# A fused attention and FFN kernel: the value products of a unit placed behind the first-layer products of their step, one half of P at a time

## The chip, the cores and the metric

The kernel runs on one core of one Trainium2 chip. The metric is device time in microseconds for one execution of the whole program.

## The reference

An attention whose mask comes from a hash, and a feed-forward network on its output, all in 32-bit floats. There are 4 batches of 8 heads, 768 positions, 64 features per head; the FFN goes from 512 to 2048 and back.

```python
q_bits = (einsum('bhsd,dk->bhsk', q, proj) > 0)      # 6 bits; k_bits likewise
mask = q_bucket[:, :, :, None] == k_bucket[:, :, None, :]
scores = where(mask, q @ k^T / 8, -1e9)
scores = scores - max(scores)
attn = exp(scores); attn = attn / (sum(attn) + 1e-09)
x = (attn @ v)  ->  [3072 tokens, 512]
h = x @ w_in
g = h * clip(h + 3, 0, 6) / 6
out = g @ w_out
```

## The kernel before, in words

**Precision.** TensorE multiplies a reduced 32-bit format, so operands are kept as a high part (rounded, written by ScalarE) and a low part (the rest, written by VectorE or POOL), and a product is made of two or three partial products that are summed in PSUM.

**Attention.** A score tile g holds 128 queries against the 768 keys of a head; there are 192 of them, six to a head. TensorE makes it with four products (L387, L389) into the PSUM tile s. VectorE copies it out and finds the row's extreme (`lowest`, L396), ScalarE takes the exponential (`exponential`, L408); the result is the tile p, the P of the title. The value products need P with the keys on the partitions. For tiles below GT = 102 TensorE transposes p (L418). From tile 102 on VectorE transposes blocks in place (`flip`, L429), SyncE's queue writes the tile to DRAM (fd) and reads it back in the other order into one of two buffers, spare and px (`move`).

**Halves.** `split_p` makes the high part ph on ScalarE (L475) and the low part pl. The 768 keys are cut in two halves of three key blocks: c = 0, whose low part VectorE makes (L479), and c = 1, whose low part POOL makes (L477; POOL's half). The halves of one unit are tiles of their own; there are two buffers for ph and two for pl, so a half of the next unit takes the buffer of the same half of this one.

**Units.** Two score tiles, 2u and 2u + 1, are a unit u: 256 queries. Its value products multiply the split v of the head (stationary) with ph and pl (moving): 2 halves x 3 key blocks x 2 parts = 12 products of 128x256, all summed into one PSUM tile, acc. `values_whole` (L505, its products at L513) issues all twelve; `values` (L500) issues half a unit at a time in the earlier part of the program. ScalarE copies acc out (`output`, L547), from where it goes to DRAM (xs) by SyncE's and POOL's queues.

**The FFN** works on chunks of 256 tokens, with 16 steps fc of 128 hidden features each. A step has 12 first-layer products of 128x256 (`gemm1`, L661) into the PSUM tile h; ScalarE's ReLU (L683) and VectorE's multiplication (L684), both from h; the split of the result into gb, high on ScalarE (L689) and low on VectorE (L690); and 6 second-layer products of 128x512 (`gemm2`, L699, L700, L704) into po, where L699 and L700 need the high part and L704 the low one. gb of a step is made at the start of the next step, and used in it.

**The order.** On TensorE, VectorE, ScalarE and POOL the order in which the code is written is the order of execution; the order on SyncE's queue is made by a scheduler. The part that the change concerns is `beside_ffn(k)`, called for k = 101 to 194: one step of attention and one step of the FFN side by side. `fill` is a coroutine over the FFN; `go("A")` to `go("D")` let it run when it has come to that stage: A splits gb, B issues the first-layer products, C the second-layer products of the step before and the gate, D side work. In a step from k = 102 on, TensorE's queue held before the change: in odd steps the 12 value products of unit (k - 3) / 2; the first-layer products; in one odd step of each head six hash products (L334 to L336); the second-layer products; the score products of tile k + 3; in some steps two transposes for the normalisation of a chunk (L587). Even steps have no value products. In step k the halves of tile k - 1 are split: POOL's half right after the exponential, the other half behind the ReLU.

**PSUM.** acc, h, the hash tile z and the normalisation tile rt come from `bank()`, which deals four banks out in turn. A tile waits for whoever still reads the bank that it is given.

Of the kernel before, what the change touches and what calls it, by code (L numbers as in the profile page):

```python
# [43 lines left out]
def lsh_attention_moe(  # L44
# [11 lines left out]
    B, H, D, S = qkT.shape  # L56
# [4 lines left out]
    QT = HW // P  # L61
# [31 lines left out]
    def bank(shape, name: str, tag: str | None = None):  # L93

        nonlocal turn
        if tag is None:
            tag = ("pt", "pu")[turn % 2]
            turn += 1
        return ps.tile(shape, F32, name=name, tag=tag, bufs=2)
# [132 lines left out]
    GT = GF + FT  # L232
# [179 lines left out]
    pts, parts = {}, {}  # L412
# [92 lines left out]
    def values_whole(u: int):  # L505
        vv = vvs[2 * u // KT]
        acc = accs[u] = bank([P, 2 * P], f"acc{u}")
        both = [parts.pop((u, c)) for c in range(2)]
        first, end = (0, 1, 0), (1, 0, QT - 1)
        for part in range(2):  # L510
            for c in (1, 0):
                for x in range(QT):
                    nc.tensor.matmul(  # L513
                        acc[:], lhsT=vv[:, c * QT + x], rhs=both[c][part][:, x],
                        start=(part, c, x) == first, stop=(part, c, x) == end,
                    )

    adds, fresh = [], []

# [552 lines left out]
    vnext = 0  # L1072

    def value_whole():
        nonlocal vnext
        values_whole(vnext // 2)
        vnext += 2

    def value_half():
        nonlocal vnext  # L1080
        u, c = divmod(vnext, 2)
        vnext += 1
        values(u, c)
        return c == 1
# [14 lines left out]
    with tc.manual_schedule(engines={ET.PE, ET.DVE, ET.Activation, ET.Pool}):  # L1099
        split_qk(0, None)  # L1100
        hash_qk(0)
        bits(0)
        scale_q(1)
        split_v(0)
        for x in range(3):
            ahead(0, x)
        for _ in range(2):
            cv(0)
        def go(part: str):
            if stage == part:  # L1110
                next(fill, None)

        through = []

        def beside_ffn(k: int):

            nonlocal paced, stage, held
            held = False  # L1120
            if k < GT:
                for c in range(2):
                    transp(k, c)
                exponential(k + 1)
            for _ in range(2):
                u = vnext // 2
                if u < NS // 2 and (2 * u < GT or k % 2 and k >= 2 * u + 3):
                    if vnext % 2 == 0 and k >= GT:
                        value_whole()
                        through.append(u)  # L1130
                        break
                    if value_half():
                        through.append(vnext // 2 - 1)
                if k < GT:
                    break
            behind = (k - 1 + LA) % KT == 4
            if GT <= k < NS - 2 and not behind:
                lowest(k + 2)
            go("A")
            if GT <= k < NS - 2 and behind:  # L1140
                lowest(k + 2)
            if k < GT:
                for c in range(2):
                    split_p(k, c, False)
                split_lows()
                while through:
                    output(through.pop(0))
                flip(k + 1)
            if k + 2 < NS:
                if k < GT:  # L1150
                    lowest(k + 2)
                    assert len(side) <= 2
                    opening.pop()()
                if k == GT:
                    go("B")
                    go("C")
                exponential(k + 2)
            paced = True
            multiply()
            if k + 2 < NS:  # L1160
                flip(k + 2)
            split = GT <= k - LT < NS
            if split:
                split_p(k - LT, 1, False)
            go("B")
            if k == NS + LT:
                homes.clear()
            while through and (through[0] < vnext // 2 - 1 or k % 2 == 0 or k < GT):
                output(through.pop(0))
            hashed = k + LA < NS and (k + LA) % KT == 4 and (k + LA) // KT + 1 < NJ  # L1170
            if hashed:
                hash_qk((k + LA) // KT + 1)
            if split:
                amid.append(lambda: (split_p(k - LT, 0, False), split_lows()))
            go("C")
            while amid:
                amid.pop()()
            split_lows()
            if hashed:
                bits((k + LA) // KT + 1)  # L1180
            if k + LA < NS:
                lead(k + LA)
            if moves:
                moves.pop(0)()
            if GT <= k + 1 < NS:
                move(k + 1)

            place_in_chunk = (k - GT) % NFC
            if subs and (k % 2 and (k < GT or place_in_chunk != NFC - 1) or k > GT and place_in_chunk == 0):
                subs.pop(0)()  # L1190
            go("D")
            if k % KT in (1, 3):
                add()

        for k in range(NS + LT + 2):
            if k >= GT - 1:
                beside_ffn(k)
                continue
            end = GB if k < GB else NS
            i, t = divmod(k, KT)  # L1200
            if k == HK - XE:
                lent += lents[cc3:]
            if k == GB:
                lent.clear()
            if k == GF - 6:
                load_first_x()
            if k == HK:
                late["x"] = sp.tile([P, S], F32, name="late", tag="raw", bufs=1)
            for c in range(2):
                transp(k, c)  # L1210
            if k + 1 < end:
                exponential(k + 1)
            if k + 2 < end:
                lowest(k + 2)
            if k == GB:
                next(first)
                pair_turn = 0

            third = True
            whole = False  # L1220
            for _ in range(1 if k != HK else 2):
                if vnext < k - k % 2:
                    whole = value_half()
            held = k >= GF - 2
            if held:
                next(fill, None)
            if whole and k >= GF:
                output(vnext // 2 - 1)
                whole = False

            hashed = k >= GF and (k + LA) % KT == 2
            after = hashed or k >= GF and (k + LA) % KT == 3
            if k >= GF and k + LA < end and not after:
                lead(k + LA)
            for c in range(2):
                split_p(k, c, third)
            split_lows()
            multiply()
            held = False
            if (k < GF or after) and k + LA < end:  # L1240
                if hashed:
                    if (k + LA) // KT + 1 < NJ:
                        hash_qk((k + LA) // KT + 1)
                        bits((k + LA) // KT + 1)
                    next(fill, None)
                lead(k + LA)
            if k == GB - 2:
                hash_qk((GB - 1) // KT + 1)
                bits((GB - 1) // KT + 1)
            if whole:  # L1250
                output(vnext // 2 - 1)
            if k >= GF - 2 and not hashed:
                next(fill, None)
            if k < GB:
                for f in early_steps[k]:
                    f()

            if k < HK and t == 1 and i:
                with tc.issue_after(last.ins):
                    load_w(i)  # L1260
            if k == HK:
                add()
                late_x()
                with tc.issue_after(last.ins):
                    get_qk(H + 2)
                    for n in range(WE, WL):
                        load_w(n)
            if k + 1 == GB:
                first = first_ffn(lambda part: ahead(GB, part))
                next(first)  # L1270
                for _ in range(2):
                    whole = value_half()
                output(vnext // 2 - 1)
                next(first)
        paced = False
        assert vnext == NS and not through
        add()
        add()
        for _ in fill:
            pass  # L1280
# [47 lines left out]
```

## Time and profile before

| | |
|---|---|
| median of 3 runs | 975.36 us (973.79 to 977.28) |
| the profiled execution's own time | 973.11 us |
| its span, first to last instruction | 971.3 us |
| instructions | 19460 |
| granted TensorE clock, mean | 0.998 |
| value products at L513 | 276 on ph and 276 on pl, from 396.2 to 812.4 us |
| bytes moved by DMA | 152.06 MB |

The rows in the prediction are of one profiled execution. A row of the timeline has the start in microseconds from the span's start, the duration, the engine, the line of the program, the operation, output and inputs, the shape, the type and how many instructions were merged into the row; in square brackets stands the idle time of that engine just before, and what ended it. PE is TensorE's matmul, PEld its weight load, DVE is VectorE, ACT ScalarE, POOL GpSimd, SP SyncE. Matmuls are pipelined: each starts before the one ahead of it has ended, and a matmul's end is modelled. A row of the waits has the waiting engine, its line, what it waited for, and then the total, the number of times and the longest wait.

### The profile page before, as it was taken

How to read it: one execution, taken by the hardware profiler on the slowest of the kernel's cores; microseconds unless marked ns; L12 is line 12 of the kernel's file. 1: busy time of each engine (PE TensorE's matmuls, PEld its weight loads, DVE VectorE, ACT ScalarE, POOL GpSimd, SP SyncE). 2: the span in 40 equal slices, each digit the busy share in tenths (PEclk: the TensorE clock that was granted, in tenths of full speed). 3: DMA queues.
4: the chain of work that ended last, by engine and by line, in shares of the span. 5: the costliest groups of instructions: out<-in, count | busy, mean ns of one | idle time of the engine just before them, and what ended most of it. 6: DMA issues, size and time to landing. Idle time of an engine off the chain costs nothing.

```text
span 971.3 us, 19460 instructions
## 1 busy us (share of the span) xinstructions
PE 948.0 (98%) x6306; PEld 873.6 (90%) x6306; DVE 723.5 (74%) x1470; ACT 625.0 (64%) x1421; POOL 473.6 (49%) x582
## 2 busy tenths in 40 slices
PE   8999999999999999899999999999999999999997
PEld 7999888999989999799899899989899899889896
DVE  7999988888569999877878878878777874342422
ACT  6898875655478988667766666666666664333332
POOL 6777744665537776455555545555545432000000
PEclk9999999999999999999999999999999999999999
DMA  3567579100035554787898788788887772101000
GB/s 117 140 156 188 131 224 377 58 1 1 6 119 119 115 142 112 192 252 233 238 267 234 231 256 241 230 267 236 243 258 233 211 227 71 44 1 44 1 22 22
DMA packets 113613, 152.06 MB, mean 157 GB/s; under 512 B 13876, under 2 KB 82612, under 8 KB 113512
## 3 DMA queue, kind: packets, MB, share of 16 engines
q1 hardware_dynamic: 108472, 144.79, 48.8%
q0 software_dynamic: 5040, 6.03, 5.3%
q8 instruction: 50, 0.82, 0.4%
q14 instruction: 51, 0.42, 0.2%
HBM read 77.34 MB, written 54.00 MB: 135 GB/s over the span
## 4 chain that ended last, share of the span: by engine, by line
PE 79%; DVE 8%; DMA 4%; ACT 4%; issue 3%; POOL 1%; SPq 1%; ACTq 0%; DVEq 0%; POOLq 0%
PE h L661 25%; PE acc L500 6%; PE po L704 6%; PE po L699 6%; PE po L700 6%; PE acc L513 6%; PE pt L418 5%; PE s L389 5%; PE s L387 5%; DMA spare<-fd 2%; DVE p L396 2%; DVE pl L479 2%; ACT ph L475 1%; SPq L78 1%; DVE qq L352 1%
## 5 line engine op out<-in xcount | busy, mean ns | idle before, releaser
L408 ACT ACTIVATE p<-p,m 128x768 f32<-128x768 f32 x192 | 180.2, 939 | 113.4 <-DVE p L396 105.2
L396 DVE TENSOR_SCALAR_CACHE_REDUCE p<-s 128x768 f32<-128x768 f32 x192 | 182.7, 952 | 24.9 <-PE pt L418 12.4
L684 DVE SCALAR_TENSOR_TENSOR h<-g,h 128x256 f32<-128x256 f32 x192 | 81.1, 423 | 102.0 <-ACT g L683 99.0
L683 ACT ACTIVATE g<-h,three 128x256 f32<-128x256 f32 x192 | 91.2, 475 | 94.9 <-PE h L661 94.0
L661 PE MATMUL h<-xh,w 128*128 128x256 f32 x1024 | 146.8, 282 | 0.0
L661 PEld LDWEIGHTS h<-xh,w 128*128 128x128 f32 x1024 | 134.9, 188 | 4.2 <-ACT xh L650 0.6
L429 DVE STREAM_TRANSPOSE p<-p 128x768 f32<-128x768 f32 x90 | 88.1, 979 | 65.2 <-ACT p L408 65.1
L477 POOL TENSOR_TENSOR pl<-spare,ph 128x384 fp32r<-128x384 f32 x45 | 45.8, 1018 | 127.3 <-ACT ph L475 71.4
L479 DVE TENSOR_TENSOR pl<-pt,ph 128x384 fp32r<-128x384 f32 x196 | 100.0, 550 | 4.0 <-ACT ph L475 3.5
L387 PE MATMUL s<-kk,qq 76*128 76x384 f32 x384 | 100.5, 343 | 2.0 <-ACT kk L357 1.5
L389 PE MATMUL s<-kk,qq 128*128 128x384 f32 x384 | 100.4, 343 | 0.0
L700 PE MATMUL po<-w,gb 128*128 128x512 f32 x250 | 98.4, 393 | 0.0
L699 PE MATMUL po<-w,gb 128*128 128x512 f32 x250 | 98.3, 393 | 0.0
L475 ACT CAST ph<-pt 128x384 fp32r<-128x384 f32 x196 | 86.1, 474 | 14.3 <-PE pt L418 13.0
L216 POOL TENSOR_TENSOR w<-wr,w 128x128 fp32r<-128x128 f32 x128 | 71.9, 593 | 45.2 <-ACT w L210 41.9
L418 PE MATMUL pt<-ident,p 128*128 128x128 f32 x612 | 86.2, 275 | 1.9 <-DVE pl L479 1.1
L689 ACT CAST gb<-h 128x256 fp32r<-128x256 f32 x141 | 52.4, 372 | 54.5 <-DVE h L684 26.8
L661 PE MATMUL h<-xl,w 128*128 128x256 f32 x512 | 81.2, 280 | 0.0
L418 PEld LDWEIGHTS pt<-ident,p 128*128 128x128 f32 x612 | 72.5, 141 | 8.9 <-PE pt L418 1.5
L704 PE MATMUL po<-w,gb 128*128 128x512 f32 x250 | 78.6, 395 | 1.5 <-DVE gb L690 1.5
L318 POOL TENSOR_TENSOR kk<-raw,qq 64x192 fp32r<-64x192 f32 (+1 forms) x73 | 65.4, 920 | 25.1 <-ACT qq L304 21.7
L387 PEld LDWEIGHTS s<-kk,qq 76*128 76x128 f32 x384 | 66.6, 190 | 11.7 <-ACT kk L357 2.0
(153 smaller groups left out, 2150.9 us busy)
## 6 DMA issues: line engine op xcount, KB each, us to landing
fd<-p SPq DMA_DIRECT2D x90, 384.0 KB
spare<-fd SPq DMA_DIRECT2D x180, 96.0 KB
px<-fd SPq DMA_DIRECT2D x180, 96.0 KB
kk<-qq SPq DMA_DIRECT2D x62, 192.0 KB
wr<-in_w_in SPq DMA_DIRECT2D x16, 512.0 KB
wr<-in_w_out SPq DMA_DIRECT2D x16, 512.0 KB
raw<-in_qkT SPq DMA_DIRECT2D x19, 384.0 KB
vr<-in_v SPq DMA_DIRECT2D x32, 192.0 KB
```

What stands on the lines that cost most here:

```text
L387: nc.tensor.matmul(s[:, c, :HW], lhsT=q1[:KM, us], rhs=half(k1[:KM], c), start=True, stop=False)
L389: nc.tensor.matmul(s[:, c, :HW], lhsT=q2[:, us], rhs=half(k2, c), start=False, stop=True)
L396: nc.vector.tensor_scalar(out=pr_[:], in0=s[:, :, :HW], scalar1=CAP, scalar2=None, op0=ALU.min, op1=ALU.min, accum_out=m[:],)
L408: nc.scalar.activation(pr_[:], pr_[:], AF.Exp, bias=m[:], scale=-1.0, accum_out=sms[b][:, t, h : h + 1])
L418: nc.tensor.transpose(pt[:, x], probs[g][0][:, c, x * P : (x + 1) * P], ident[:])
L475: nc.scalar.copy(hi, pt)
L479: lows.append(lambda: engine.tensor_sub(lo, pt, hi.bitcast(F32)))
L661: nc.tensor.matmul(hp, lhsT=wi[:, wp, wc], rhs=x[cc][xp], start=(k == 0 and cc == 0), stop=(k == 2 and cc == NCC - 1),)
L683: nc.scalar.activation(r[:], hp, AF.Relu, bias=three[:], scale=1.0)
L699: nc.tensor.matmul(po[u], lhsT=gh[:, us], rhs=wo[:, 0], start=(fc == 0), stop=False)
L700: nc.tensor.matmul(po[u], lhsT=gh[:, us], rhs=wo[:, 1], start=False, stop=False)
L704: nc.tensor.matmul(po[u], lhsT=gl[:, us], rhs=wo[:, 0], start=False, stop=(fc == NFC - 1))
```

## The change

`values_whole` no longer issues the twelve products itself; it allocates acc and returns a function that issues one half: its three high products, then its three low ones. `value_whole` puts the work on a list, `rest`. For the one unit whose score tiles lie below GT (unit 50) it runs at once, at its old place. For the other 45 units, 51 to 95, it runs behind `go("B")`, so behind the first-layer products of the same step; POOL's half (c = 1) goes first, then the other. The split of POOL's half of the next tile, which was written ahead of `go("B")`, is written behind it, because it reuses the buffers that the moved products read.

```diff
     def values_whole(u: int):
         vv = vvs[2 * u // KT]
         acc = accs[u] = bank([P, 2 * P], f"acc{u}")
-        both = [parts.pop((u, c)) for c in range(2)]
         first, end = (0, 1, 0), (1, 0, QT - 1)
-        for part in range(2):
-            for c in (1, 0):
+
+        def half(c: int):
+            both = parts.pop((u, c))
+            for part in range(2):
                 for x in range(QT):
                     nc.tensor.matmul(
-                        acc[:], lhsT=vv[:, c * QT + x], rhs=both[c][part][:, x],
+                        acc[:], lhsT=vv[:, c * QT + x], rhs=both[part][:, x],
                         start=(part, c, x) == first, stop=(part, c, x) == end,
                     )
+
+        return half
...
     def value_whole():
         nonlocal vnext
-        values_whole(vnext // 2)
+        u = vnext // 2
+
+        def whole():
+            half = values_whole(u)
+            for c in (1, 0):
+                half(c)
+
+        rest.append(whole)
+        if vnext < GT:
+            rest.pop()()
         vnext += 2
+
+    rest = []
...
             split = GT <= k - LT < NS
+            go("B")
+            while rest:
+                rest.pop()()
             if split:
                 split_p(k - LT, 1, False)
-            go("B")
             if k == NS + LT:
                 homes.clear()
```

On TensorE at unit 59 (step k = 121), before the change: s123 is the score tile of the step before, ph59_1 and pl59_1 are POOL's half of the unit, ph59_0 and pl59_0 the other, h1_1_3 is the first layer of the FFN step, z21 the hash of head 21.

```order
L387 MATMUL s123_6721<-kk_20_6143,qq_20_6144 128x384 x2
L389 MATMUL s123_6721<-kk_20_6143,qq_20_6144 128x384 x2
L513 MATMUL acc59_6731<-ph59_1_6637,vv19_6407 128x256 x3
L513 MATMUL acc59_6731<-ph59_0_6663,vv19_6407 128x256 x3
L513 MATMUL acc59_6731<-pl59_1_6638,vv19_6407 128x256 x3
L513 MATMUL acc59_6731<-pl59_0_6664,vv19_6407 128x256 x3
L661 MATMUL h1_1_3_6758<-xh1_1_6546,w6_2339 128x256 x8
L661 MATMUL h1_1_3_6758<-xl1_1_6547,w6_2339 128x256 x4
L334 MATMUL z21_0_6771<-qq_21_6534,pjl_74 108x384
```

And the same place with the change (line numbers behind the diff are higher, so L513 became L514 and L661 became L664):

```order
L387 MATMUL s123_6721<-kk_20_6143,qq_20_6144 128x384 x2
L389 MATMUL s123_6721<-kk_20_6143,qq_20_6144 128x384 x2
L664 MATMUL h1_1_3_6741<-xh1_1_6546,w6_2339 128x256 x8
L664 MATMUL h1_1_3_6741<-xl1_1_6547,w6_2339 128x256 x4
L514 MATMUL acc59_6754<-ph59_1_6650,vv19_6407 128x256 x3
L514 MATMUL acc59_6754<-pl59_1_6651,vv19_6407 128x256 x3
L514 MATMUL acc59_6754<-ph59_0_6663,vv19_6407 128x256 x3
L514 MATMUL acc59_6754<-pl59_0_6664,vv19_6407 128x256 x3
L334 MATMUL z21_0_6771<-qq_21_6534,pjl_74 108x384
```

The twelve value products moved behind the twelve first-layer products, and POOL's low part moved ahead of the other half's high part. The orders on ScalarE, VectorE and POOL are the same as before, instruction by instruction. On SyncE's queue twelve places differ by a transfer or two; this is the difference at step k = 114, where fd116 is the write of a transposed tile, xs2 that of a unit's output y18_0, and spare and px are the buffers that transposed tiles are read into:

```order
 L78 DMA spare_5091<-fd114_6173 32x4x192 x4
 L78 DMA raw21_6326<-in_qkT 64x768 x2
+L78 DMA fd116_6296<-p116_6288 128x768
 L78 DMA xs2_127<-y18_0_6190 64x512
-L78 DMA fd116_6296<-p116_6288 128x768
-L78 DMA px_5555<-fd115_6236 32x4x192 x4
-L78 DMA fd117_6364<-p117_6356 128x768
+L78 DMA px_5555<-fd115_6223 32x4x192 x4
+L78 DMA fd117_6351<-p117_6343 128x768
```

Here the write of the transposed tile went ahead of the write of y; the rows of px and fd117 differ only in the numbers of their buffers.

## The prediction

> **What bounds the kernel now.** I read the page first, then the busy time of the stage that the change touches (microseconds 412 to 814), then that stage's waits, then the timeline around single units. The page's first part:
>
> ```profile
> PE 948.0 (98%) x6306; PEld 873.6 (90%) x6306; DVE 723.5 (74%) x1470; ACT 625.0 (64%) x1421; POOL 473.6 (49%) x582
> ```
>
> TensorE is the bound; no other engine is near. What can be won is only time in which TensorE itself stands. The stage by itself, from the view of busy time by stretch (span, PE, PEld, DVE, ACT, POOL, then granted clock, DMA share, GB/s):
>
> ```profile
> 412.00:814.00 402.00, 397.54 (x2591) 367.90 (x2592) 313.87 (x601) 267.01 (x625) 208.69 (x269) 1.00 0.81 237
> ```
>
> The granted clock is 1.00, so no time hides there. PE shows 4.5 us of idle time, and the waits of this stage (total, times, longest) say where most of it is, and how often VectorE has to wait for TensorE:
>
> ```profile
> DVE p L396 <- PE s L389: 8.2, 21, 0.6
> ...
> PEld acc L513 <- ACT ph L475: 6.0, 12, 1.7
> ...
> PE acc L513 <- ACT ph L475: 4.5, 9, 1.5
> ```
>
> TensorE's idle time lies ahead of the value products (L513), which wait for ScalarE's high part of P. Here is a unit without such a wait (59), and VectorE's wait for a score tile in the even step before it:
>
> ```profile
> 481.12 0.96 DVE L396 TENSOR_SCALAR_CACHE_REDUCE p<-s 128x768 f32<-128x768 f32 x1 [0.42 <-PE s L389]
> ...
> 483.19 0.98 DVE L429 STREAM_TRANSPOSE p<-p 128x768 f32<-128x768 f32 x1 [0.76 <-ACT p L408]
> ...
> 483.46 0.36 ACT L547 COPY y<-acc 128x256 f32<-128x256 f32 x1
> ...
> 484.07 0.52 PE L389 MATMUL s<-kk,qq 128*128 128x384 f32 x2
> ...
> 484.43 0.88 PE L513 MATMUL acc<-ph,vv 128*128 128x256 f32 x6
> ...
> 485.86 1.10 PE L661 MATMUL h<-xh,w 128*128 128x256 f32 x8
> ...
> 487.04 0.50 ACT L475 CAST ph<-spare 128x384 fp32r<-128x384 f32 x1
> ...
> 487.53 0.48 ACT L683 ACTIVATE g<-h,three 128x256 f32<-128x256 f32 x1
> ...
> 488.31 0.40 PE L699 MATMUL po<-w,gb 128*128 128x512 f32 x1
> ```
>
> From first value product to first first-layer product: 485.86 - 484.43 = 1.43 us for twelve products, 0.12 each. Now unit 66, with two rows of the step pair before it:
>
> ```profile
> 541.49 0.63 PE L661 MATMUL h<-xl,w 128*128 128x256 f32 x4
> ...
> 542.22 0.48 ACT L683 ACTIVATE g<-h,three 128x256 f32<-128x256 f32 x1 [0.43 <-PE h L661]
> ...
> 548.55 0.52 PE L389 MATMUL s<-kk,qq 128*128 128x384 f32 x2
> ...
> 549.41 1.00 POOL L477 TENSOR_TENSOR pl<-px,ph 128x384 fp32r<-128x384 f32 x1 [4.00 <-ACT ph L475]
> 549.47 0.59 PE L513 MATMUL acc<-ph,vv 128*128 128x256 f32 x3 [0.39 <-ACT ph L475]
> ...
> 549.86 0.51 ACT L475 CAST ph<-px 128x384 fp32r<-128x384 f32 x1
> ...
> 550.40 0.56 DVE L479 TENSOR_TENSOR pl<-px,ph 128x384 fp32r<-128x384 f32 x1
> 550.42 0.62 PE L513 MATMUL acc<-ph,vv 128*128 128x256 f32 x3 [0.36 <-ACT ph L475]
> ...
> 551.59 1.10 PE L661 MATMUL h<-xh,w 128*128 128x256 f32 x8
> ...
> 551.97 0.36 ACT L689 CAST gb<-h 128x256 fp32r<-128x256 f32 x1
> ...
> 552.99 0.39 PE L699 MATMUL po<-w,gb 128*128 128x512 f32 x1
> ```
>
> In unit 59 the first value product follows 0.36 us after the first of the two score products (484.07), so unit 66 should have begun at 548.91; it began 0.55 us late and then took 551.59 - 549.47 = 2.12 us instead of 1.43: together 1.24 us, where the idle column shows 0.39 + 0.36. I use the distance from start to start, since the next product's start is what the path feels. By the idle column's 4.5 us the gain would be 2 us after what comes back below, and the time 973.
>
> **The change, part by part.** *Waits removed.* The 45 moved units, first and last:
>
> ```profile
> 412.03 1.31 PE L513 MATMUL acc<-ph,vv 128*128 128x256 f32 x6 [0.57 <-ACT ph L475]
> ...
> 413.92 0.28 PE L661 MATMUL h<-xh,w 128*128 128x256 f32 x1
> ...
> 811.09 0.87 PE L513 MATMUL acc<-ph,vv 128*128 128x256 f32 x6
> ...
> 812.51 0.75 PE L661 MATMUL h<-xh,w 128*128 128x256 f32 x5
> ```
>
> Over them, (start of the first first-layer product) - (start of the first value product) - 1.43 sums to 9.7 us. Ten units follow a pair of transposes and need 1.50 without any wait (456.31 to 457.82 below), so 0.7 of it is no wait: 9.0. Ahead of the first product, units 51, 66 and 90 wait 0.73, 0.55 and 0.54: 1.8. Gross: **10.8 us**. Seven units (51, 63, 66, 74, 75, 87, 90) hold 7.4 of it.
>
> Do the waits go? The moved products start 1.43 us later against ScalarE, and are ordered POOL's half high, POOL's half low, other half high, other half low: operands are needed at +1.43, +1.79, +2.14 and +2.50. Take unit 66, its start at 548.91: POOL's low part ends at 550.41 (needed 550.70), ScalarE's other high part at 550.37 (needed 551.05), VectorE's low part at 550.96 (needed 551.41). All in time, in one of the worst three units.
>
> *What is late next.* TensorE now reaches the second-layer products (L699) earlier by what it no longer waits, and their operand gb comes from ScalarE, which is not earlier. In unit 66 gb is there 0.66 us before its use (551.97 + 0.36 against 552.99), and TensorE is 1.24 us ahead, more with what it carries from units 63 and 64: 0.6 to 1.0 comes back. Unit 75:
>
> ```profile
> 632.26 0.51 PE L513 MATMUL acc<-ph,vv 128*128 128x256 f32 x3
> ...
> 633.07 0.37 ACT L547 COPY y<-acc 128x256 f32<-128x256 f32 x1 [1.10 <-DMA xs<-y]
> ...
> 634.25 0.56 DVE L479 TENSOR_TENSOR pl<-px,ph 128x384 fp32r<-128x384 f32 x1
> 634.27 0.63 PE L513 MATMUL acc<-ph,vv 128*128 128x256 f32 x3 [1.50 <-ACT ph L475]
> ...
> 634.85 0.36 ACT L689 CAST gb<-h 128x256 fp32r<-128x256 f32 x1
> 635.45 1.10 PE L661 MATMUL h<-xh,w 128*128 128x256 f32 x8
> ...
> 636.85 0.39 PE L699 MATMUL po<-w,gb 128*128 128x512 f32 x1
> ```
>
> It loses 635.45 - 632.26 - 1.43 = 1.76, because ScalarE waits for a transfer; the margin of gb is 1.64 and the lead would be 1.76 plus 0.6 from unit 74: 0.7 comes back there, and 0.3 in the step after. VectorE regains about 0.4 of lateness per pair of steps (8.2 us over 21 waits), so leads under that die out. For two more units (70, 90) I put 0.4 together. Given back: 0.8 + 1.0 + 0.4 = 2.2, say **2.4**; bounds 0 (all engines follow) and 7.4 (all seven late units only move their wait).
>
> *ScalarE's cast behind the moved products.* The next unit's high part for POOL's half reuses the buffer that the first three moved products read. In unit 59 this cast starts at 487.04, 2.61 after the unit. The products' result: +1.43, three products 0.24 to the third's start, and from a product's start to ScalarE's use 0.38 (the fourth of the products from 541.49 starts at 541.84, L683 at 542.22): +2.05. Covered by 0.56; nothing. Behind that cast stand the ReLU (L683), the other cast and gb, and their readers on VectorE. The ReLU itself starts at +3.10 right behind the cast, so an earlier h brings nothing in such a unit. A rule speaks against this part of the change: the Trainium skill (PSUM — Partial Sum Buffer, section "Engine vs sequencer instructions") states that ScalarE's queue is strict first in, first out and that matmuls complete in program order, so a cast that waits for products moved back by 1.43 us stops all of ScalarE. The trace agrees in unit 75 above, where one late copy (L547) holds what follows; by the rows the cast is not late and the term is 0, and where it were late the second rival gives the time.
>
> *Banks.* In ten units, where transposes take banks too, the first-layer products now wait for the copy of the unit before (L547) out of acc. In unit 56:
>
> ```profile
> 454.99 0.36 ACT L547 COPY y<-acc 128x256 f32<-128x256 f32 x1
> ...
> 456.31 0.96 PE L513 MATMUL acc<-ph,vv 128*128 128x256 f32 x6
> ...
> 457.82 1.10 PE L661 MATMUL h<-xh,w 128*128 128x256 f32 x8
> ```
>
> It ends 0.96 before; these units have little lead (0.3 at most of their own): nothing, 0 to 0.3 each, up to 2 us in all.
>
> *Queues.* The orders of ScalarE, VectorE and POOL stay as they are, POOL's transfers too. On SP some neighbours change place; where the write of a transposed tile (fd) goes ahead of that of y, y waits for the transpose: it ends at 484.17, the copy at 483.82, so 0.35 us. The next copy into a y buffer is a whole pair of steps off: nothing.
>
> *Sum.* 10.8 - 2.4 = 8.4 us. The profiled execution took 973.11 (span 971.3) and would take 964.7; the median of the runs shown is 2.25 above it, so the forecast is 975.36 - 8.4 = **967.0 us**.
>
> **Rivals.** *The wait moves on.* If ScalarE and VectorE, not TensorE's order, set the pace in the late units, the seven give back all: 10.8 - 7.4 = 3.4, so 972.0. For it: the casts in 66 and 75 are late because ScalarE had other work or a transfer to wait for, which stays. Against: only 66 and 75 have a gb margin smaller than the lead; and ACT is busy 267 of 402 us. Chance 0.20.
>
> *ScalarE is held by the moved products: slower.* If results reach ScalarE later than the 0.38 of the row, the cast at +2.61 waits, and everything behind it in ScalarE's queue. VectorE regains 0.4 a pair, so from +3.0 on each further 0.1 us costs 45 x 0.1 = 4.5 us. The loss exceeds the gain's 8.4 by the measurable 2.9 when the products reach ScalarE at +3.25; at +3.3 it is 13.5 us lost, 5 us net, 980.5. Against: that is 1.2 us later than the row's price. Chance 0.05.
>
> That the change does not do what it says is excluded by the order on TensorE. Another cause that I do not see: 0.02.
>
> **How the numbers follow.** Forecast 0.73. 0.3% of this kernel, 2.9 us, is about what a measurement can tell from no change. The low end takes all 10.8 and 1 us of scatter in the runs: 963.5. The high end takes the first rival whole: 972.0. The first rival lies at that bound, so half of its 0.20 counts as the same: faster 0.73 + 0.10 = 0.83, same 0.11, slower 0.06.
>
> **What would show it.** In the profile after: L514's idle time (the value products' new line) near 1 us, where L513 had 10.5 in PE and PEld together; TensorE's busy share of the same steps near 100%; a wait of the second-layer products for gb in units 66 and 75 and hardly elsewhere; ScalarE's cast still at +2.6 after the step's start in units like 59. I am wrong if the value products still wait, if second-layer products wait in many units (first rival), or if ScalarE's cast waits for acc in most steps (second).

## The result, and the profile after

Six runs of each kernel on one chip: 967.95 us with the change (median; 966.79 to 970.6), 976.32 before (973.79 to 978.29). The ratio is 0.9914, 95% interval 0.9892 to 0.9935: 8.4 us faster. The profiled execution of the change took 969.05 us (span 967.3) and that of before 973.11 (971.3), so this pair differs by only 4.0 us. The profile of before is faster than each of its timed runs on that chip, and that of the change is slower than its median by 1.1; a sum made from one pair of traces has that uncertainty.

The page's first part and the stage from 412 to 814 us with the change, in the same columns as before:

```profile
PE 945.9 (98%) x6306; PEld 871.8 (90%) x6306; DVE 722.2 (75%) x1470; ACT 623.5 (64%) x1421; POOL 474.4 (49%) x582
...
412.00:814.00 402.00, 400.35 (x2618) 370.36 (x2619) 315.20 (x606) 268.49 (x632) 211.03 (x272) 1.00 0.81 238
```

PE is busy for 400.35 of 402 us, where it was 397.54. Its idle time fell from 4.5 to 1.7 us. The value products by themselves: the view of one source line tells what its engines sat idle for (microseconds, times; products and weight loads are counted each, and "issue" is idle time for which the profile shows no cause), first with the change (L514), then before (L513):

```profile
  ACT ph L475: 0.7, 2
  DVE pl L479: 0.2, 1
```

```profile
  ACT ph L475: 10.5, 21
  issue: 2.2, 3
...
```

What TensorE waits for now, from the view of waits between 412 and 813 us (total, times, longest):

```profile
PEld h L664 <- DVE qq L352: 1.7, 4, 0.7
...
PEld po L702 <- ACT gb L692: 1.3, 3, 0.7
PEld po L707 <- DVE gb L693: 1.2, 4, 0.5
...
PE po L702 <- ACT gb L692: 0.7, 2, 0.5
```

These are small, and they stand at other products: the second layer waits for gb, and the first layer waits for VectorE's hash bits (L352). The second of these is not in the prediction.

Unit 59 with the change. The step starts at 483.71, where the first-layer products now come first:

```profile
483.71 1.10 PE L664 MATMUL h<-xh,w 128*128 128x256 f32 x8
...
485.11 0.52 PE L514 MATMUL acc<-ph,vv 128*128 128x256 f32 x3
...
485.37 0.94 ACT L408 ACTIVATE p<-p,m 128x768 f32<-128x768 f32 x1 [0.98 <-DVE p L396]
...
486.30 0.50 ACT L475 CAST ph<-spare 128x384 fp32r<-128x384 f32 x1
...
486.70 0.47 ACT L686 ACTIVATE g<-h,three 128x256 f32<-128x256 f32 x1
```

ScalarE's cast starts 486.30 - 483.71 = 2.59 after the step, without a wait: the exponential ahead of it (L408) ends there. By the prediction's arithmetic the moved products had freed its buffer at 485.11 + 0.24 + 0.38 = 485.73. In the stage's waits no cast of ScalarE waits for acc in this profile; in the second profile of the change one does, for 0.2 us. Unit 66, the one with a named price:

```profile
549.14 0.52 PE L514 MATMUL acc<-ph,vv 128*128 128x256 f32 x3
...
549.50 0.52 PE L514 MATMUL acc<-pl,vv 128*128 128x256 f32 x3
...
549.85 0.52 PE L514 MATMUL acc<-ph,vv 128*128 128x256 f32 x3
...
550.21 0.52 PE L514 MATMUL acc<-pl,vv 128*128 128x256 f32 x3
...
550.78 0.36 ACT L692 CAST gb<-h 128x256 fp32r<-128x256 f32 x1
...
551.19 0.50 PE L702 MATMUL po<-w,gb 128*128 128x512 f32 x1 [0.46 <-ACT gb L692]
```

All four groups of value products follow one another at 0.36 us; then the second-layer product waits for gb. Without the wait it would have started 0.36 after 550.21, so 551.19 - 550.57 = 0.62 us are lost.

**All profiles side by side.** For every product on TensorE between 380 and 820 us I took the distance from the start of the one before, less the usual distance for that pair of shapes, and added up what is over 0.05 us, by the product that came late (microseconds; the kernels further down are explained there):

| kernel | value products | first layer | second layer | transposes (L587) | span |
|---|---|---|---|---|---|
| before | 11.5 | 3.6 | 2.3 | 1.4 | 971.3 |
| before_again, the same | 12.7 | 3.6 | 2.2 | 1.4 | 972.5 |
| the change | 1.0 | 6.2 | 5.4 | 1.9 | 967.3 |
| again, the same | 0.3 | 5.0 | 5.2 | 1.6 | 965.0 |
| move_only | 0.8 | 5.3 | 4.0 | 1.6 | 964.7 |
| order_only | 16.0 | 3.9 | 2.6 | 1.4 | 976.0 |
| held | 0.1 | 22.1 | 7.5 | 5.3 | 988.9 |
| held_bits | 0.1 | 7.9 | 7.8 | 1.4 | 971.6 |

In ten units 0.085 us behind a pair of transposes is booked on whichever product comes next. That 0.85 moves from the first column to the second with the change and is no wait.

### The profile page after: what moved, and what is told of

Read it like the earlier page. It is cut to its first block, busy times and chain, and to the rows that moved or that the text cites. A ratio compares the mean times of both kernels' runs of the same rounds, so it can differ in the third digit from the quotient of the medians.

```text
span 967.3 us, 19453 instructions
## 1 busy us (share of the span) xinstructions
PE 945.9 (98%) x6306; PEld 871.8 (90%) x6306; DVE 722.2 (75%) x1470; ACT 623.5 (64%) x1421; POOL 474.4 (49%) x582
## 4 chain that ended last, share of the span: by engine, by line
PE 83%; DVE 8%; DMA 4%; issue 2%; ACT 2%; POOL 1%; SPq 1%; DVEq 0%; ACTq 0%; POOLq 0%
PE h L664 26%; PE po L702 7%; PE po L707 7%; PE po L703 7%; PE acc L500 6%; PE acc L514 6%; PE s L389 5%; PE s L387 5%; PE pt L418 5%; DVE p L396 2%; DVE pl L479 2%; DMA fd<-p 1%; DVE qq L352 1%; PE rt L590 1%; PE z L336 1%
## 5 line engine op out<-in xcount | busy, mean ns | idle before, releaser
L408 ACT ACTIVATE p<-p,m 128x768 f32<-128x768 f32 x192 | 180.1, 938 | 114.4 <-DVE p L396 100.4
L396 DVE TENSOR_SCALAR_CACHE_REDUCE p<-s 128x768 f32<-128x768 f32 x192 | 182.3, 950 | 18.7 <-PE pt L418 11.7
L664 PE MATMUL h<-xh,w 128*128 128x256 f32 x1024 | 147.3, 283 | 0.8 <-DVE qq L352 0.4
L664 PEld LDWEIGHTS h<-xh,w 128*128 128x128 f32 x1024 | 136.6, 188 | 5.5 <-DVE qq L352 1.7
L479 DVE TENSOR_TENSOR pl<-pt,ph 128x384 fp32r<-128x384 f32 x196 | 100.0, 550 | 3.9 <-ACT ph L475 3.5
L702 PE MATMUL po<-w,gb 128*128 128x512 f32 x250 | 98.9, 396 | 0.7 <-ACT gb L692 0.7
L475 ACT CAST ph<-pt 128x384 fp32r<-128x384 f32 x196 | 86.0, 473 | 14.7 <-PE pt L418 13.4
L664 PE MATMUL h<-xl,w 128*128 128x256 f32 x512 | 81.7, 280 | 0.0
L387 PEld LDWEIGHTS s<-kk,qq 76*128 76x128 f32 x384 | 66.4, 189 | 11.5 <-ACT kk L357 2.0
```

The source lines that it names most:

```text
L387: nc.tensor.matmul(s[:, c, :HW], lhsT=q1[:KM, us], rhs=half(k1[:KM], c), start=True, stop=False)
L396: nc.vector.tensor_scalar(out=pr_[:], in0=s[:, :, :HW], scalar1=CAP, scalar2=None, op0=ALU.min, op1=ALU.min, accum_out=m[:],)
L408: nc.scalar.activation(pr_[:], pr_[:], AF.Exp, bias=m[:], scale=-1.0, accum_out=sms[b][:, t, h : h + 1])
L479: lows.append(lambda: engine.tensor_sub(lo, pt, hi.bitcast(F32)))
L664: nc.tensor.matmul(hp, lhsT=wi[:, wp, wc], rhs=x[cc][xp], start=(k == 0 and cc == 0), stop=(k == 2 and cc == NCC - 1),)
L702: nc.tensor.matmul(po[u], lhsT=gh[:, us], rhs=wo[:, 0], start=(fc == 0), stop=False)
```

## The experiments

All are timed against the kernel before on their own chip. The first four shared a chip (before: 974.6 us, 972.62 to 978.72). My theory at the outset was that of the prediction: TensorE stood ahead of value products whose operands were late, and it is their place behind the first-layer products that hides this. The rivals were that the order of the halves does it, and that ScalarE is close to being held by the moved products.

**again: the change a second time, no edit.**

> The changed kernel once more, for a second profile and more runs. My theory (operands come just in time; the moved products need them 1.43 us later) expects 968, between 966 and 970, and value products whose idle time stays near 1 us. The theory that the lateness only moves on expects a second profile in which the waits for gb and for h's bank add up to as much as the value products lost before (10 us), and a gain under 4 us.

Measured: 967.48 us (966.18 to 969.55), ratio 0.9924 (0.9903 to 0.9945), 7.1 us faster. The value products' waits were gone again, in unit 75 too. There ScalarE's copy of y still waits for a transfer, but less long. The copy in the first profile, then in this one:

```profile
631.22 0.37 ACT L550 COPY y<-acc 128x256 f32<-128x256 f32 x1 [1.73 <-DMA xs<-y]
```

```profile
629.37 0.37 ACT L550 COPY y<-acc 128x256 f32<-128x256 f32 x1 [1.15 <-DMA xs<-y]
```

Behind the first the value products of unit 75 lost 0.72 us, behind the second 0.10.

**order_only: the new order of the halves, at the old place.** `rest` is emptied where the work is put on it, and `split_p` of POOL's half stands ahead of `go("B")` again:

```diff
         rest.append(whole)
-        if vnext < GT:
-            rest.pop()()
+        rest.pop()()
...
-            go("B")
-            while rest:
-                rest.pop()()
             if split:
                 split_p(k - LT, 1, False)
+            go("B")
```

> The new order of the halves at the old place, ahead of the first-layer products. My theory: POOL's low part is then needed 0.36 us after the start instead of 0.71, where it ends at 0.3 to 0.95, so the value products wait more, not less: 8.8 us by the ends of the four parts in the profile of before become 12.1, so 3 us slower than before, 979 (976 to 981). The rival that the order of the halves brings the gain expects 968 to 972.

Measured: 979.14 us (977.8 to 980.14), ratio 1.004 (1.0027 to 1.0053): slower than before by 4. What the engines sat idle for ahead of the value products (L514):

```profile
  POOL pl L477: 12.0, 32
  ACT ph L475: 4.2, 5
  issue: 2.2, 3
...
```

At the old place POOL's low part, now wanted second and not third, is late: it holds up 21 weight loads and 11 products, the 32 of the row. The order of the halves by itself does harm there.

**move_only: the old order (both high parts, then both low), at the new place.** `half` now takes the part, and runs over both halves of P itself:

```diff
-        def half(c: int):
-            both = parts.pop((u, c))
-            for part in range(2):
+        both = [parts.pop((u, c)) for c in range(2)]
+
+        def half(part: int):
+            for c in (1, 0):
...
-            for c in (1, 0):
-                half(c)
+            for part in range(2):
+                half(part)
```

> The old order of the twelve products, all behind the first-layer products. My theory: with 1.43 us more, either order finds its operands ready, except in the one unit where ScalarE waits for a transfer, and there the last low part decides in both: the same as the change, 968 (966.5 to 969.5). The rival that the order of the halves matters expects at most half the gain, 972 or more.

Measured: 966.59 us (966.35 to 969.04), ratio 0.9916 (0.9897 to 0.9935). It can't be told from the change (967.48 on the same chip). The place brings the whole gain, as far as these runs can tell. At that place nearly all operands are there in either order; what is left ahead of the value products stands in unit 75:

```profile
  ACT ph L475: 1.2, 2
```

**held: the other half of P only behind the second-layer products.** This makes ScalarE's cast for that half late, which prices the second rival. `rear` is a second list, and what is still on it behind `go("C")` runs there:

```diff
-            for c in (1, 0):
-                half(c)
+            half(1)
+            if vnext <= GT:
+                half(0)
+            else:
+                rear.append(lambda: half(0))
...
-                amid.append(lambda: (split_p(k - LT, 0, False), split_lows()))
+                amid.append(lambda: ([rear.pop()() for _ in rear[:]], split_p(k - LT, 0, False), split_lows()))
```

> As the change, but the other half (c = 0) of the value products stands behind the second-layer products, so the cast into its buffer, at about +3.5 us of the step, waits for products whose result comes at +4.2 us, and VectorE's low part behind it likewise. This makes the wait that my second rival feared. My theory: VectorE and ScalarE regain about 0.4 us a pair of steps, so some 0.3 of the 0.7 us reach TensorE in each of 45 units: 13 us slower than the change, 981, bounds 972 and 990. If ScalarE's waits are hidden altogether: 967 to 969, as the change. If each goes through in full: 45 x 0.7 = 31 us, 999.

Measured: 990.79 us (990.64 to 991.55), ratio 1.016 (1.0138 to 1.0183). That is 23 us slower than the change, more than I had expected and just outside the bounds. The waits of its stage (412 to 835 us):

```profile
ACT ph L475 <- PE acc L514: 26.7, 24, 2.0
...
PE h L664 <- DVE qq L352: 11.5, 13, 1.4
...
PE rt L590 <- DVE qq L352: 3.4, 3, 1.4
```

ScalarE waits 24 times for the value products, as it was made to. But what TensorE itself waits for is something else: the hash bits, once a head. The step of unit 59 shows the chain:

```profile
490.43 0.34 PE L336 MATMUL z<-qq,pjh 128*108 128x384 f32 x1
...
490.45 0.47 ACT L686 ACTIVATE g<-h,three 128x256 f32<-128x256 f32 x1
...
492.34 0.52 PE L514 MATMUL acc<-pl,vv 128*128 128x256 f32 x3
...
492.60 0.51 ACT L475 CAST ph<-spare 128x384 fp32r<-128x384 f32 x1 [1.68 <-PE acc L514]
...
493.06 0.52 PE L389 MATMUL s<-kk,qq 128*128 128x384 f32 x2
493.14 0.56 DVE L479 TENSOR_TENSOR pl<-spare,ph 128x384 fp32r<-128x384 f32 x1 [1.67 <-ACT ph L475]
...
493.73 1.29 DVE L352 TENSOR_SCALAR qq<-z,thr,val 44x384 fp32r<-44x384 f32 x2
...
494.57 1.18 PE L664 MATMUL h<-xh,w 128*128 128x256 f32 x8 [0.99 <-DVE qq L352]
```

The cast waits 1.68 us for its buffer. VectorE's low part (L479) waits for the cast, and in VectorE's queue the hash bits stand behind the low part, though the last product of z started at 490.43. The first-layer products need z's bank, and TensorE stands for 0.99 us (1.15 from start to start). Of the 14 losses of over 1 us that TensorE has in this stage, 13 end with the bits. The Trainium skill (PSUM — Partial Sum Buffer, section "Engine vs sequencer instructions") says that ScalarE's queue is strictly first in, first out. The trace agrees: nothing ran on ScalarE in those 1.68 us. What such a wait costs depends on who stands behind it.

The next four runs shared another chip (before: 975.12 us, 973.26 to 976.25).

**before_again: a second profile of the kernel before, no edit.**

> The kernel before, a second profile. My theory: the value products' waits belong to their place, so they come again whatever the transfers do: summed from start to start 10 to 12 us, own time 974 to 978. Rival (most of those waits were an accident of the transfers in the one profile shown): 6 us or less, in other units than 51, 63, 66, 74, 75, 87 and 90.

Measured: 974.25 us in the profiled execution. The waits for the casts come again in size (11.7 us of idle time in 23 waits of products and weight loads, against 10.5 in 21) and mostly in place: the seven late units of the prediction hold 7.4 us of start-to-start loss again, with unit 75 again the longest, 1.75 us. Single waits of another unit come and go (unit 77 loses 0.60 here and nothing in the first profile). So most of them belong to the order of the program, not to one execution's transfers.

**xr_after: a transfer kept where it was on SyncE's queue.** In the change the write of a transposed tile (fd) at the start of the stage stands behind one more read of chunk (1,1) than before. Before and with the change, SyncE's fd, VectorE's next L396, and the second-layer product that waits for the low gb behind it:

```profile
403.39 0.53 SPq L78 DMA_DIRECT2D fd<-p  x1
...
403.72 0.96 DVE L396 TENSOR_SCALAR_CACHE_REDUCE p<-s 128x768 f32<-128x768 f32 x1 [0.45 <-DMA fd<-p]
...
405.08 0.73 PE L704 MATMUL po<-w,gb 128*128 128x512 f32 x2 [0.80 <-DVE gb L690]
```

```profile
404.04 0.53 SPq L78 DMA_DIRECT2D fd<-p  x1
...
405.10 0.96 DVE L396 TENSOR_SCALAR_CACHE_REDUCE p<-s 128x768 f32<-128x768 f32 x1 [1.53 <-DMA fd<-p]
...
406.46 0.73 PE L707 MATMUL po<-w,gb 128*128 128x512 f32 x2 [1.88 <-DVE gb L693]
```

```diff
-                pieces.append(lambda cc=cc: dma(out=xr[:, cc], in_=of[:, cc]))
+                def one(cc=cc):
+                    if (b, t) != (1, 1):
+                        return dma(out=xr[:, cc], in_=of[:, cc])
+                    with tc.issue_after(last.ins):
+                        dma(out=xr[:, cc], in_=of[:, cc])
+
+                pieces.append(one)
```

> The change, with the four input transfers of chunk (1,1) kept behind the write of a transposed tile on SyncE's queue, where they stood in the kernel before at that place. My theory: the change in SyncE's order makes VectorE wait for its tile at 405 and TensorE for gb at 406 (2.0 and 1.3 us lost from start to start in two profiles of the change, 1.0 before): with this the loss there falls to 1.0 or less and the time to 966.2 to 967.2, 0.3 to 1.3 us under the change's 967.5. Rival (the wait at 405 has another cause, the order on the queue costs nothing): the loss at 406 stays at 1.3 or more and the time at 967.5.

Measured: 967.8 us (966.24 to 969.86), ratio 0.9925 (0.9912 to 0.9938). The wait fell as expected:

```profile
406.13 0.73 PE L713 MATMUL po<-w,gb 128*128 128x512 f32 x2 [0.24 <-DVE gb L699]
```

0.41 us are lost there from start to start, where the change lost 2.04 and 1.32 in its two profiles. The time did not fall: the change itself did not run on this chip, but its ratios to the kernel before, 0.9914 and 0.9924 on two others, stand against 0.9925 here. So the theory holds for the wait, and no gain shows in the time. A gain of 1 us is smaller than what the runs of one kernel differ by (3.6 us here).

**bits_first: the hash bits ahead of the low part, in the change.**

```diff
-                amid.append(lambda: (split_p(k - LT, 0, False), split_lows()))
+                early = hashed and stage == "C"
+                amid.append(lambda: (split_p(k - LT, 0, False), early and bits((k + LA) // KT + 1), split_lows()))
...
-            if hashed:
+            if hashed and not (split and early):
```

> The change, with the two hash-bit instructions (L352) of the hash steps on VectorE ahead of the low part of the other half. My theory: with the products moved, the first-layer products wait in several units for the bank that the hash tile z holds until its bits are made (0.3 us or more each at 571, 599, 654 and 736, about 1.2 together); with earlier bits these waits go and the time falls to 966.3 to 967.2. Rival: the low part comes later by the two instructions and the value products wait for it instead, so the sum stays the same: 967.5, or up to 1 more.

Measured: 968.22 us (966.85 to 970.28), ratio 0.9931 (0.9918 to 0.9944). The wait of the first layer for the bits is gone (1.7 + 0.4 us in the change's profile, none here). In its place TensorE waits longer for what VectorE makes next:

```profile
PEld po L707 <- DVE gb L693: 3.1, 6, 1.1
...
PE po L707 <- DVE gb L693: 1.2, 3, 0.6
```

With the change the first of these was 1.2, and the second does not show. The rival was right that the sum stays and wrong about the place: not the value products but the second layer waits now. In these steps VectorE's order chose who waits. SyncE's order changed along with it in some sixteen places; that this cost nothing is not shown.

**both: the two edits together.**

> The change with both edits, the four transfers kept back and the hash bits earlier. My theory: both gains come, since they lie in different steps: 965.2 to 966.7. Rival (neither loss is real or each turns into another wait): 967.5.

Measured: 968.43 us (967.24 to 970.29), ratio 0.9934 (0.9922 to 0.9947). No gain shows, alone or together.

**held_bits: held, with the hash bits ahead of the low part.** The edit is that of bits_first, in the held kernel. The orders on TensorE, ScalarE and POOL stay those of held; on SyncE's queue some fifteen transfers stand elsewhere, nearly all of them those into kk, which move up. By then my theory had changed. The prediction had priced a late cast by its own lateness, all of it beyond what VectorE regains going through to the time. The held profile suggested that the price is paid at the hash tile's bank alone.

> The held kernel (the other half's six products behind the second-layer products, 990.8 us) with the two hash-bit instructions on VectorE ahead of the low part of the other half. In the held profile TensorE's losses of over 1 us stand almost all in the step after a hash step, once per head, where the first-layer products wait 1.0 to 1.4 us for the bank of the hash tile. My new theory: ScalarE's late cast costs little by itself and is regained within the pair of steps; it costs where VectorE's hash bits stand behind the low part that waits for that cast, and TensorE needs the bank. With the bits ahead these waits go: 970 to 977 us, 14 to 20 under the held kernel. Rival (the prediction's pricing: each late cast moves the whole order, whatever waits for it): the losses only change their place, 987 to 991.

Measured: 973.95 us (972.22 to 974.96), ratio 0.9981 (0.9971 to 0.9991) to before at 975.26 (973.15 to 977.67). The waits of its stage (412 to 833 us) and unit 59 again:

```profile
ACT ph L475 <- PE acc L514: 25.4, 23, 2.0
```

```profile
488.05 0.34 PE L336 MATMUL z<-qq,pjh 128*108 128x384 f32 x1
...
489.12 1.29 DVE L352 TENSOR_SCALAR qq<-z,thr,val 44x384 fp32r<-44x384 f32 x2
...
490.22 0.51 ACT L475 CAST ph<-spare 128x384 fp32r<-128x384 f32 x1 [1.68 <-PE acc L514]
...
490.68 0.52 PE L389 MATMUL s<-kk,qq 128*128 128x384 f32 x2
...
490.76 0.56 DVE L479 TENSOR_TENSOR pl<-spare,ph 128x384 fp32r<-128x384 f32 x1 [0.34 <-ACT ph L475]
...
491.04 1.10 PE L664 MATMUL h<-xh,w 128*128 128x256 f32 x8
```

The cast waits the same 1.68 us, and ScalarE's waits over the stage are nearly the same (25.4 us against 26.7). But the bits are made while VectorE would have waited, and TensorE follows without idle time. Of held's loss 16.8 us vanish (17.5 when each kernel is taken against the kernel before on its own chip). The two-instruction swap that gave nothing in the change is worth that much where the low part is late.

## Why the prediction came out right, and where its steps were off

Forecast 967.0 in a range of 963.5 to 972.0; measured 967.95, and 967.48 on a second chip. The difference of 8.4 us forecast stands against 8.4 and 7.1 measured. That the first agrees to the tenth is luck: the second chip gave 1.3 less, and the two pairs of profiles 5.8 on the mean.

- **Waits removed, 10.8 us: right.** The value products' stalls fell from 11.5 and 12.7 to 1.0 and 0.3. Less the 0.85 that only changed its row, that is 10.6 on the mean of two profiles each. move_only shows that the place does it and order_only that the order does not. Measuring from start to start was needed: by the idle column's 4.5 us PE could not have gained 7 to 8.
- **ScalarE's cast, 0: right.** +2.59 without a wait, forecast +2.6.
- **gb in unit 66, 0.6 to 1.0: right**, 0.62 in both profiles of the change. **Unit 75, 1.0: near in size once, at another place.** In the first profile of the change 0.72 was lost there at the value products themselves and 0.21 at the second layer, in the second 0.10 and 0.21. The prediction had tested the operands in unit 66 alone and booked all of unit 75's loss on gb. The copy that holds ScalarE there waited 1.10 and 1.16 us in the two profiles of before, 1.73 and 1.15 in those of the change.
- **Given back, 2.4 in all: under-sized in the traces.** There the second layer loses 3.1 us more than before (5.3 against 2.2 on the means), the first layer 5.6 - 3.6 - 0.85 = 1.1, the transposes 0.3: 4.5 together. The net of the traces is then 10.6 - 4.5 = 6.1, where the spans differ by 5.8 on the means. The runs' medians leave 10.6 - 8.4 = 2.2 to 10.6 - 7.1 = 3.5 for the same term. Which of these is nearer stays open: one profile of a kernel scatters by 2 us and more.
- **Where it is given back: in good part elsewhere.** Of the second layer's 3.1, units 66 and 75 hold 0.9 and the product at 406 us 0.7 on the mean; the steps of units 70 and 90 hold nothing. Much of the rest is at 718.97 in the first profile (0.5) and at 644.78 and 646.19 in the second (1.4), in steps without value products, behind casts (L475) that had waited 1.60 and 1.37 us. The view names old products of TensorE as what ended these two waits; their real cause stays open.
- **Banks, 0 to 2: the size right, the holder wrong.** I had looked at the copy out of acc (L547). TensorE, now earlier, runs into the bank of the hash tile, which VectorE's bits (L352) release. The copy did hold a bank in unit 56 of xr_after, for 0.3 us.
- **SyncE's order, nothing: not shown to be right.** One swap delayed a tile's write and cost 0.3 to 1.1 us at 406 (1.3 and 2.0 against 1.0 before), and xr_after takes it away there; in the time this can't be seen.
- **The rivals.** The first (the seven late units give back 7.4) did not come: of the seven only units 66 (0.7) and, in one profile, 75 (0.9) still lost over 0.5. The second named a mechanism that exists, and its condition was not reached. Its price was wrong, though: 4.5 us per 0.1 of lateness from +3.0 on, with VectorE regaining 0.4 a pair. In held_bits ScalarE waits 25.4 us in 23 casts, 1.1 us on the mean, and the kernel is only some 6 us slower than the change. In held nearly the same waits come with a loss of 23, 16.8 of it by VectorE's order in one step a head. By the rival's own rule, which lets through what a wait has beyond 0.4, they would have cost 17 in both.

## What to carry to other kernels

Where the bound engine stops for an operand that is a little late in a few places, put work whose operands are long ready ahead of it; the place decides, and a finer order of the late work can even do harm (order_only). Price a late instruction by what stands behind it in the queue of each engine that waits for it, down to the release that the bound engine needs: the same 1.68 us of waiting cost 1.15 us or nothing, depending on two instructions of VectorE. Here, with the bound engine over 99% busy in the stage, clearing waits of about 1 us brought no gain that runs with a scatter of 3 us could show.

## What the runs showed of the hardware

- Late products held ScalarE for 25 us of a 421 us stage, in waits of up to 2.0 us, and the kernel, bound by TensorE, was slower than the change by about 6 (held_bits); with another order of VectorE's low part and hash bits it was 23 (held).
- TensorE's idle column understates a stall: 0.46 us idle ahead of the L702 product at 551.19 was 0.62 from start to start, 0.24 ahead of L713 at 406.13 was 0.41, and 0.99 ahead of L664 at 494.57 was 1.15.
- Executions of one and the same kernel differed by up to 6 us (972.62 to 978.72 for the kernel before on one chip, 966.79 to 970.6 for the change), and two profiles of the change by 2.3 in span. A wait for a transfer can differ between them: the copy in unit 75 waited 1.73 and 1.15 us.
